# RWKV-7 scan with a gelu MLP on one core: the channels of both halves moved side by side, with one transfer in place of two for three tensors

## The chip, the core and the metric

The kernel runs on one core of a Trainium2 chip. The metric is device microseconds (us) of one execution; lower is better. The page and the views shown come from one profiled execution.

## The reference, cut to what matters

Four sequences (batch B = 4) with eight heads (H = 8) of 40 channels (D = 40) run 768 steps. Each head has a 40 x 40 state, which every step reads, decays and updates; the outputs of the eight heads, 320 numbers for each token, go through an MLP with 2048 hidden units.

```python
for t in range(S):                                   # S = 768
    y[:, :, t] = np.einsum('bhd,bhde->bhe', rt, state)
    Sa = np.einsum('bhde,bhe->bhd', state, at)
    state_decay = state * wt[:, :, None, :] - np.einsum('bhd,bhe->bhde', Sa, bt)
    state = state_decay + np.einsum('bhd,bhe->bhde', vt, kt)
...
x = attn_out.transpose(0, 2, 1, 3).reshape(B * S, H * D)     # 3072 x 320
h = x @ w_in                                                 # 320 x 2048
g = h * (1.0 / (1.0 + np.exp(-1.702 * h)))
return g @ w_out                                             # 2048 x 320
```

## The kernel before

**Units.** Time is cut into 12 chunks of 64 steps, and the batch into two pairs of sequences. A pair in a chunk is a unit; there are 24, i = 0 to 23, with c, p = divmod(i, 2). In a unit the recurrence over 64 steps becomes matrix products: score matrices A, N and RV of 64 x 64 for each head, the inverse of a triangular matrix in five levels (`ps_level`), and products with the state that the unit before left. After the two units of a chunk follows that chunk's MLP: `ps_up`, a gelu on ScalarE (ACT), `ps_down`.

**Halves.** SBUF and PSUM have 128 partitions, and the kernel works on two halves of 64 (`HALF`). The tiles with time on the partitions (`time`, `logw`, `RV`) fill both halves. The tiles with channels on the partitions (`ak`, `b`, `rv`, and the sums `FT`, `GT` of the log decays) use 40 partitions of each half, 0 to 39 and 64 to 103 (`CHANNELS`), one half for the heads with e = 0 and one for those with e = 1. Almost every matmul is a 64 x 64 product that uses one quarter of the array, and `QUARTERS` goes round the four quarters so that four such products run side by side. Everything is fp32, and each product is two records in the trace. All matmuls go through the helper `mm` (L300), so they are told apart by tile: `ps_A`, `ps_N`, `ps_B` and so on.

**Transfers.** All come from the SP queue. For each unit `load` (L495) fetches `ak` (the inputs a and k), `b` and `rv` as two transfers each, of 40 partitions, and `RV` and `time` as one transfer each of 128 partitions; `load_w` (L490) fetches the decays. `part_with` (L967) stores a unit's output `x` to DRAM as two transfers of 40 partitions, and `get_back` (L973) loads it again in the layout of the MLP. `weight` (L429) fetches and converts the weights of the MLP in eight pieces, four transfers each, early in the run.

**Sums of the decays.** For the first four units (`BY_PE = 4`) the sums over time by channel are products on TensorE: `by_channel` (L550) makes 16 products of 64 x 64 with 65 columns (`ps_cumc`). From unit 4 on, VectorE scans make them.

**Products over channels.** `score_A` (L630), `score_N` (L680), the part of `known` (L884) with `zr` and `ak`, and `state_turned` (L857) contract over the 40 partitions of `CHANNELS`.

**Order.** The order of the work is written out by hand: `ORDER` lists all 2700 steps with engine and PSUM bank, and each engine takes its steps in that order. A wait of one step holds back what stands behind it on its engine. In the built program eight semaphores serve the transfers in turn, and the issue of a transfer waits until the one eight places before it has landed; so at most eight are on the way.

Of the kernel before, what the change touches and what calls it, by code (L numbers as in the profile page):

```python
# [107 lines left out]
0s 5s 7s 8s 9s 3a 6s 87p0 88p1 24s 89a1 1s 2s 12s 102a 95d 100p2 90a0 93d 158a 101d2 98p3 96g 10s 94d 17s 97g 16s 99d3 103p1  # L108
4a 11s 132p0 104a1 105d1 142p2 26s 143p3 133a0 106d 130p1 14s 144a3 13s 107p0 15s 18s 151g 108a0 109d0 51s 131a1 110p3 27s
149g 150d 111a3 112d3 159p0 156p1 145a2 161d0 160a0 152g 113p3 345s 92a 162d 25s 153d 114a3 163p2 42s 115d3 34s 19a 274s 264p0  # L110
165d2 265p3 164a2 22d 266a3 166p2 20d 273s 21d 33s 43s 167a2 154p3 168d2 23g 35s 28a 157d1 116p2 155d3 169p1 117a2 118d2 267a0
279d 63s 280g 119p3 277s 171d1 36s 44s 120d3 343s 125d3 278g 124d3 29d 126p2 170a1 123a3 30d 172p1 122a3 127a2 121a 31d 128p2
54s 173a1 287a 288p0 289a0 129d2 32g 174d1 134p3 147s 37a 290d0 175p2 135d3 180a2 146s 178a2 275s 176d2 136p1 179a2 479s 38d
181a2 45s 39d 177a 282g 291d 91s 138a1 182p0 188p3 281d 183a0 186p2 139d 137a1 283p0 187a2 184p1 189a3 40d 276s 292p2 46a
284d0 41g 285p3 185d1 344s 148a 286d3 190p0 293a2 294d2 334p1 335p3 357a 140s 191d0 268g 336a3 315d 192p2 47d 337a1 348d 316p0
194a2 295p3 349d 61s 317a0 195g 60s 347s 358p1 296a3 62s 297d3 360d1 318a0 298p3 271a 361d 319p0 338g 300d3 196s 193a2 320a0
346s 355p2 385d 270s 48d 299a3 362p0 356d2 351g 301p3 363a0 364d0 350g 269s 141s 386p2 197s 302d3 365p0 387a2 352g 359a1 303d3
388a2 323p1 367d0 366a0 321p3 49d 324a1 304p2 322a3 478s 325d1 50g 353p0 309a2 470p3 354d0 209p1 307a2 210p1 310a2 305d2 211p1
308a2 272d 198p0 341a 199p0 72s 212p1 70s 64a 200p0 340s 368p2 52s 342d 339s 69s 201p0 369a2 202p0 370d2 203p0 471a 213p1 65d
214p1 389p2 66d 472a3 483g 204p0 390a2 560s 371p3 67d 306a 53s 215p1 71s 482s 216p1 372a3 217p1 476a 220p2 373d3 68g 218p1  # L120
221p2 477d 219a1 205p0 222p2 206p0 223p2 224p2 207p0 55a 311p3 225p2 79s 312d3 80s 226p2 208a0 58d 313p1 374p3 314d1 227p2 56d
379a3 228p2 229p2 57d 326p0 230a2 59g 393p1 327d0 378a3 391p2 394a1 375d3 231p0 558s 392d2 376a 232p0 233p0 395d1 559s 81s 73a
78s 234p0 480s 381p2 235p0 328p1 481s 382a2 74d 377a3 485d 380a3 236p0 75d 492a 242p2 486d 243p2 82a 76d 484d 77g 383p3 237p0
384d3 244p2 329d1 330d1 488p3 473d 238p0 531d 245p2 487g 246p2 489d3 85d 532p1 239p0 533a1 396p3 331d 332s 474s 475s 534a1
240p0 247p2 397d3 562s 241a0 535p1 83d 490p3 536a1 84d 398p0 572a 491d3 86g 550p1 555s 561s 253p3 399d0 551a 333s 400d0 254p3
401d 402s 554s 255p3 552a1 564d 493p0 705s 556a 567g 570p1 403s 494d0 248p2 563d 566g 249p2 495d0 498d 256p3 571d1 565g 250a2
496a0 251d2 252s 696p1 497g 557d 539p0 537p2 704s 257p3 538a2 540d0 258p3 553d 611d 697a 499d 573p2 784s 700s 259p3 576a2
574d2 710d 260p3 541d0 575d2 404p0 578d 261a3 577g 405p0 579d 698a1 568p2 711g 500p1 406p0 569d2 501a1 407p0 262d3 263s 708s
580p2 702a 502d1 408p0 582d2 409p0 503d 410p0 583d 504a 612p3 411p0 584g 613d3 412p0 614d3 413p0 505p1 709d 414a0 426p3 506d1
427p3 428p3 507d1 429p3 699d 581d2 430p3 615p1 785s 706s 701s 703d 431p3 616a1 585p0 432p3 508d 586a0 433p3 587d0 434p3 509a  # L130
588d 435p3 589d 448p2 436a3 510p1 590p0 511a1 449p2 592d0 591a0 512d1 415p3 513d 416p3 593d 514a 417p3 594g 418p3 515p0 419p3
516a0 517d0 595p1 518d 420p3 596a1 597d1 421p3 598d 422p3 519a 599d 423p3 424p3 520p0 425a3 437p1 521d0 438p1 523d0 522g 439p1
524d0 440p1 525d0 441p1 442p1 526d0 527p3 718p0 929s 528a3 443p1 719d0 787s 444p1 720d0 529p3 445p1 721d0 446p1 530d3 600p0
723d 447a1 542p3 722d 724g 603d0 605a0 619p1 604d0 543d3 450p2 620a1 606d0 544p3 621d1 601d0 602d 617p1 707s 546d3 451p2 618a1
783s 712d 547g 713d 607p0 725p1 608a0 452p2 609p0 453p2 548s 610d0 932s 454p2 727d1 726d1 622p0 728d 545d3 729a 775p1 455p2
623d0 780s 776a 549s 756d 730p3 624p0 456d2 457d2 731d3 458s 459p2 777a1 778g 732d3 786s 788g 781a 779s 626d0 460p2 625d0 627g
733d 795p1 835d 734a 461p2 735p3 791g 462p2 628s 736a3 796d1 737d3 716p0 792g 738d 463p2 782d 739g 1011s 920p1 757p3 925s
464p2 717d0 758a3 629s 759a3 790d 465p2 740p0 789d 466p2 741a0 742d0 921a 797p3 467d2 760p0 1008s 468d2 800a3 923d 652p2 469s
761d0 922a1 653p2 926a 930s 798d3 714p1 799d3 654p2 924s 802d 801g 655p2 934d 803a 656p2 836p0 657p2 715d1 658p2 659p2 837d0
762p3 838d0 927d 660p2 763a3 661p2 764p1 662a2 743d 630p0 744d 928s 631p0 632p0 765d1 804p3 766d1 633p0 805a3 806d3 634p0 807d  # L140
635p0 808a 745p2 636p0 748d2 637p0 749d2 839p1 933g 750d2 638p0 840a1 1009s 751d2 639p0 809p3 746d2 935g 640a0 641p1 810d3
642p1 793p2 747a 811d3 674p0 812d 794d2 813a 752p3 643p1 753a3 814p2 644p1 815a2 816d2 754p3 645p1 755d3 646p1 817d 647p1 818a
767p2 841p3 768d2 648p1 842a3 649p1 819p2 650p1 820a2 821d2 675p0 769p3 822d 651a1 823d 771d3 931s 770d3 772g 824p2 936d 676p0
827a2 828a2 942p1 829a2 677p0 1153s 830a2 937d 945a1 773s 663p3 825d2 664p3 943d1 1156s 826a 665p3 944d1 999p2 947d 946g 666p3
1000a 1004s 980d 940p1 948g 667p3 941d1 668p3 774s 669p3 670p3 831p1 671p3 1001a2 1002d 1003s 832d1 672p3 1005a 1013d 678p0
673a3 1006d 833p2 843p1 679p0 834d2 1007s 844d1 938p2 845d1 680p0 939d2 846p3 681p0 847d3 949p1 1012g 682d0 848p2 950a1 683d0
1014d 684s 685p3 849d2 1015g 1010s 850d2 1021p0 1016g 951d1 686p3 1024a0 1232s 851d 1235s 981p2 687p3 982a2 952d 852s 1022d0
983a2 953g 1144p1 1023d0 688p3 1026d 1145a 1149s 1025d 1027g 984p2 1059d 689p3 1154s 954p0 853s 985a2 1147g 690p3 1158d 1148s
955a0 956d0 986p2 1146a1 957d 1150a 691p3 958d 987a2 1151d 988p0 692p3 989a0 1152s 990d0 959p1 693a3 865p2 960a1 694d3 866p2
961d1 867p2 695s 962d 868p2 963d 1028p0 869p2 1029a0 1030d0 870p2 1031d 1157g 871p2 1159d 1032a 1060p3 872p2 873p2 1061a3  # L150
874p2 1062d3 1033p1 875a2 854p0 1035d1 855p0 1036d 856p0 1037d 1063p3 857p0 1064d3 1034a1 858p0 964p2 859p0 965a2 966d2 1038p1
967d 860p0 1039a1 1040d1 861p0 1041d 1017p3 968a 1042g 862p0 1018d3 863p0 969p2 864a0 876p1 970d2 877p1 972d2 971g 1043p3
973d2 878p1 1044a3 974d2 879p1 975d2 880p1 881p1 1045d3 1019p0 1046d 976p2 1047a 882p1 1020d0 1233s 883p1 977a2 1166p3 884p1
1169a3 1167d3 1377s 978p0 885p1 1168d3 898p2 1171d 1170g 886a1 979d0 887p3 1172a 1048p0 991p1 1051a0 888p3 1052a0 992d1 889p3
1053a0 890p3 1054a0 891p3 1049d0 993p1 1050a 1067p0 994d1 1160g 1155s 892p3 1161d 1068a0 893p3 894p3 1069d0 1380s 895p3 1204d
1065p0 995d1 896p3 996d 1066a0 1231s 1055p1 899p2 897a3 1056d1 997s 1173p0 1223p3 900p2 1174a0 1175d0 1228s 1176d 1224a 1177g
1057p1 901p2 1058d1 1070p0 998s 1164p1 1225a3 1226d 1236g 1227s 1071d0 902p2 1229a 1165d1 1162p3 903p2 1238d 1163d3 904p2
1237d 1178p0 1230d 905p2 1179a0 1180d0 1245p1 906a2 1181d 1072p3 1248a1 1456s 907d2 1182g 1246d1 908s 1247d1 909p0 1250d 1234s
1239g 1073d3 1251a 910p0 1240g 1074d3 1249d 1183p2 1459s 1283d 1368p1 911p0 1184a2 1075d 1373s 912p0 1185d2 1369a 1076s 1186d
1252p3 1187d 913p0 1370a1 1371g 1372s 1382d 1253a3 1188p2 1254d3 1374a 914p0 1255d 1190d2 1256g 1077s 1189a2 1191d 1243p1  # L160
1375d 915p0 1192g 1257p3 916p0 1244d1 1258a3 1259d3 1205p2 917d0 1206a2 1193p1 918d0 1207a2 1089p3 1260d 919s 1196a1 1090p3
# [87 lines left out]
def rwkv7_gelu_quick(ctx: ExitStack, tc: tile.TileContext, time_d, v_d, w_d, wc_d, ak_d, b_d, rv_d, w_in, w_out, out):  # L249
# [12 lines left out]
    WALK = "ebufbub"  # L262
    EARLY = 4
    BY_PE = 4
    PLAIN = 4
    PARTS = 4
    ROUNDS, WINDOW, SHARE = 4, 5000.0, 1.0
    RANKS = [14, 16, 20, 24, 35, 37, 39, 41]
# [97 lines left out]
    for t in logw_t:  # L366
        nc.gpsimd.memset(t[:, DM:], 0.0)
# [770 lines left out]
```

## Time and profile before

| | |
|---|---|
| time, median of 3 runs | 677.02 us (676.87 to 680.05) |
| span of the profiled execution, first to last instruction | 676.5 us |
| PE busy | 648.5 us, 96% of the span |
| PE matmul records | 19488 |
| granted clock of PE, mean | 0.994 |
| DMA | 35313 packets, 69.74 MB |

PE is TensorE's matmuls, PEld its weight loads, DVE VectorE, ACT ScalarE, POOL GpSimd, SP SyncE; SPq is SP's queue of transfer issues. The span was 0.5 us under the median of the runs. "Idle before" is the time for which an engine stood still ahead of an instruction, with what ended it; "issue" there means that the profile shows nothing that was waited for. PEclk is the granted share of TensorE's full clock.

### The profile page before, as it was taken

What the parts mean: (1) busy time and instruction counts of PE and PEld (TensorE: products, weight loads), DVE (VectorE), ACT (ScalarE), POOL (GpSimd) and SP (SyncE); (2) the same over time, 40 slices, a digit from 0 to 9 for tenths busy, and PEclk for the clock granted to TensorE, in tenths of its full rate; (3) what the DMA queues carried; (4) which work ended last, traced back from release to release, by engine and by line L of the source; (5) the groups of instructions that cost most, each with busy time, mean ns of one, the idle gap of its engine ahead of it and who ended that gap; (6) DMA issues with size and microseconds to landing.
All of it is one profiled execution on the core that took longest, in us unless ns stands there. A gap on an engine that the chain in (4) does not pass through costs nothing.

```text
span 676.5 us, 42217 instructions
## 1 busy us (share of the span) xinstructions
PE 648.5 (96%) x19488; PEld 553.4 (82%) x19488; DVE 444.6 (66%) x908; ACT 331.6 (49%) x710; POOL 175.3 (26%) x204
## 2 busy tenths in 40 slices
PE   5768999999999999999999999999999999999997
PEld 5657887987998987788888888798888798798785
DVE  4786787777867667767776587768656766675001
ACT  4676755534564655664545445455454354252110
POOL 6344244224123123123123211322412421300000
PEclk9899999999999999999999999999999999999999
DMA  7983736315314314432404413513412411200200
GB/s 230 300 289 94 232 107 187 103 43 154 108 47 149 93 58 117 121 108 72 118 22 132 141 34 109 156 33 108 140 39 71 122 53 54 61 14 15 61 12 20
DMA packets 35313, 69.74 MB, mean 103 GB/s; under 512 B 5440, under 2 KB 14656, under 8 KB 35136
## 3 DMA queue, kind: packets, MB, share of 16 engines
q1 hardware_dynamic: 35136, 67.03, 32.6%
q8 instruction: 153, 2.51, 1.5%
q14 instruction: 24, 0.20, 0.1%
HBM read 59.15 MB, written 7.86 MB: 99 GB/s over the span
## 4 chain that ended last, share of the span: by engine, by line
PE 93%; DMA 2%; DVE 2%; issue 1%; ACT 1%; DVEq 0%; SPq 0%; ACTq 0%
PE ps_up L300 31%; PE ps_down L300 30%; PE ps_level L300 9%; PE ps_y L300 5%; PE ps_B L300 5%; PE ps_X L300 2%; PE ps_N L300 2%; PE ps_rz L300 2%; PE ps_RV L300 2%; PE ps_A L300 2%; PE ps_zT L300 1%; DMA ak<-in_ak 1%; PE ps_cum L300 1%; PE ps_T L300 1%; DMA b<-in_b 1%
## 5 line engine op out<-in xcount | busy, mean ns | idle before, releaser
L300 PE MATMUL ps_up<-xT_all,w_sb 64*64 64x256 f32 x3840 | 251.0, 377 | 0.8 <-issue 0.4
L300 PE MATMUL ps_down<-w_sb,g 64*64 64x320 f32 x3072 | 237.0, 430 | 0.2 <-ACT zr L877 0.2
L300 PEld LDWEIGHTS ps_up<-xT_all,w_sb 64*64 64x64 f32 x3840 | 170.1, 133 | 15.9 <-issue 1.5
L300 PEld LDWEIGHTS ps_down<-w_sb,g 64*64 64x64 f32 x3072 | 128.0, 133 | 42.8 <-ACT zr L877 0.4
L996 ACT ACTIVATE g<-ps_up 128x1024 f32<-128x1024 f32 x48 | 49.2, 1024 | 45.4 <-PE ps_up L300 45.0
L715 POOL TENSOR_TENSOR EX<-ES,quads 128x512 f32<-128x512 f32 x29 | 38.3, 1322 | 112.7 <-DVE ES L708 74.9
L300 PEld LDWEIGHTS ps_level<-W,EX 64*64 64x64 f32 x2560 | 57.8, 134 | 6.7 <-DVE T L838 0.5
L758 ACT COPY W<-ps_level 128x512 f32<-128x512 f32 (+1 forms) x56 | 29.5, 527 | 67.7 <-PE ps_level L300 65.7
L760 DVE TENSOR_TENSOR E<-two,ps_level 128x256 f32<-128x256 f32 x80 | 33.1, 415 | 34.2 <-ACT W L758 30.1
L300 PE MATMUL ps_level<-W,EX 64*64 64x64 f32 (+1 forms) x2560 | 55.4, 217 | 0.1
L713 ACT ACTIVATE EX<-ES,quads 128x256 f32<-128x256 f32 x80 | 36.3, 501 | 31.0 <-DVE ES L708 30.3
L619 POOL TENSOR_TENSOR ak<-ak,FT 128x512 f32<-128x512 f32 x16 | 20.9, 1305 | 76.6 <-DMA ak<-in_ak 53.4
L708 DVE STREAM_TRANSPOSE ES<-E 128x256 f32<-128x256 f32 x80 | 35.3, 443 | 4.4
L300 PE MATMUL ps_level<-PT,EX 64*64 64x64 f32 (+2 forms) x1280 | 32.8, 235 | 5.1 <-DVE EX L729 3.7
L300 PEld LDWEIGHTS ps_level<-PT,EX 64*64 64x64 f32 x1280 | 30.8, 139 | 8.3 <-DVE EX L729 4.2
L300 PE MATMUL ps_y<-M,bh 64*64 64x104 f32 (+1 forms) x768 | 35.6, 250 | 0.7 <-DVE M L915 0.4
L300 PE MATMUL ps_y<-RV,kh 64*64 64x104 f32 (+1 forms) x768 | 35.6, 251 | 0.0
L899 ACT COPY B<-ps_B 128x416 f32<-128x416 f32 (+1 forms) x34 | 16.6, 492 | 33.4 <-PE ps_B L300 33.2
L300 PEld LDWEIGHTS ps_y<-RV,kh 64*64 64x64 f32 x768 | 28.3, 137 | 2.6 <-DVE M L915 0.5
L689 DVE COPY_PREDICATED PT<-within,ps_N 128x256 f32<-128x256 uint32 x40 | 17.8, 444 | 18.5 <-ACT P L697 13.5
L915 DVE TENSOR_TENSOR M<-ps_X,later 128x832 f32<-128x832 f32 (+1 forms) x24 | 23.8, 993 | 8.3 <-PE ps_X L300 8.1
L300 PE MATMUL ps_B<-RV,A 64*64 64x104 f32 (+1 forms) x768 | 27.9, 252 | 1.1 <-issue 1.1
(131 smaller groups left out, 1088.2 us busy)
## 6 DMA issues: line engine op xcount, KB each, us to landing
ak<-in_ak SPq DMA_DIRECT2D x48, 160.0 KB
rv<-in_rv SPq DMA_DIRECT2D x48, 160.0 KB
time<-in_time SPq DMA_DIRECT2D x24, 320.0 KB
xT_all<-x_dram SPq DMA_DIRECT2D x48, 160.0 KB
wc<-in_wc SPq DMA_DIRECT2D x20, 264.0 KB
logw<-in_w SPq DMA_DIRECT2D x24, 160.0 KB
RV<-in_v SPq DMA_DIRECT2D x24, 160.0 KB
b<-in_b SPq DMA_DIRECT2D x48, 80.0 KB
```

What stands on the lines that cost most here:

```text
L300: nc.tensor.matmul(o, lhsT, rhs, start=start, stop=True, skip_group_check=True)
L619: plan.add(R, {"DVE": 690.0, "POOL": 1270.0, "sbuf": True}, lambda t: of(t.engine).tensor_mul(ahT(), ahT(), FT_of(i)), reads=T("ak", "FT") ...
L689: plan.add(R, dve(256), lambda t, n=n: nc.vector.copy_predicated(tiles_of(at(E0_t, i)), every(within_of(n), [128, 2, 4, 32]), blocks(psum( ...
L708: plan.add(rank, dve(256), lambda t: nc.vector.transpose(ES(n), source(t)), writes=[key("ES", n, 6)], **reads)
L713: nc.scalar.activation(dst[:, :, h], ES(n), ACT.Copy, scale=quads[:, h, :1])
L715: of(t.engine).tensor_mul(dst, ES(n).unsqueeze(2).to_broadcast([128, 8, 2, 32]), quads.unsqueeze(1).to_broadcast([128, 8, 2, 32]))
L758: plan.add(rank, any2(512 - 8 * past), lambda t: copy(t.engine)(tiles_of(W(n + 1))[:, :, :, past:], blocks(psum(t, ""), 64)[:, :, :, past: ...
L760: plan.add(rank, dve(256), lambda t: nc.vector.tensor_sub(tiles_of(E(n + 1)), every(two32, [128, 2, 4, 32]), blocks(psum(t, ""), 64)[:, :, ...
L899: plan.add(R, any2(4 * wide), lambda t: copy(t.engine)(dst(), some(psum(t, "")[:, :, :208])), writes=[("Bv", i)] if x and c > 0 else T("B" ...
L915: plan.add(R + 1, dve(8 * wide), lambda t: nc.vector.tensor_tensor(M_of(i)[:, :, :wide].rearrange("p (j b) n -> p b j n", b=2), some(psum( ...
L996: plan.add(-45, {"ACT": 1030.0, "table": "gelu"}, lambda t: nc.scalar.activation(g_of(c * NQ + q).rearrange("p m r n -> p r m n"), psum(t, ...
```

## The change

The channels of the two halves move next to each other: in `ak`, `b`, the sums of the decays, the state and the output, e = 0 lies on partitions 24 to 63 and e = 1 on 64 to 103 (`MIDDLE`, 80 partitions). The inputs are laid out so on the host. `ak` and `b` are loaded with one transfer of 80 partitions each, and `x` is stored with one. `rv` keeps its place and its two transfers.

Products over channels contract over the whole half of 64 partitions, 24 of which hold zeros in one of the factors. `by_channel` makes 8 products of 64 x 128 in place of 16 of 64 x 64. To have zeros on both sides of the channels, `logw`, `kh`, `bh` and `zT` get gaps of 24 columns, and `kh` and `bh` are written as 4 x 80 columns in place of 8 x 40. The three `logw` buffers become one tile with two fills in place of three.

The order is the same 2700 entries; the text of `ORDER` is only broken into lines at other places. The functions of the MLP were written anew with a switch (`BY_HALF = 0`) that leaves their instructions as they were.

Instruction by instruction, SP issues 342 rows in place of 414 (24 each of `ak`, `b` and `x` go), PE loses 32 products of `ps_cumc` (64 records), POOL one fill, and DVE and ACT keep all theirs. Apart from the waits on transfers no instruction waits for another step than before, but that the first `ps_cumc` product of unit 0, and no longer the sixth, waits for the fill of `logw`.

```diff
+    GAP = 24
+    MIDDLE = slice(GAP, GAP + 2 * D)
...
-    logw_t = several("logw", [128, DM + 24])
-    for t in logw_t:
-        nc.gpsimd.memset(t[:, DM:], 0.0)
+    logw_all = single("logw", [128, plan.slots["logw"] * (GAP + DM) + GAP])
+    by_slot = logw_all[:, :-GAP].rearrange("p (s n) -> p s n", n=GAP + DM)
+    nc.gpsimd.memset(by_slot[:, :, :GAP], 0.0)
+    nc.gpsimd.memset(logw_all[:, -GAP:], 0.0)
...
-    kh_t, bh_t = several("kh", [128, 8, 64]), several("bh", [128, 8, 64])
-    for t in kh_t + bh_t:
-        nc.gpsimd.memset(t[:, :, D:], 0.0)
+    def spaced(name):
+        wide = several(name, [128, 5, 128])
+        for t in wide:
+            nc.gpsimd.memset(t[:, :, :2 * GAP], 0.0)
+        return [t.rearrange("p j n -> p (j n)")[:, GAP:GAP + 512].rearrange("p (j n) -> p j n", n=64) for t in wide]
...
-            rows = [slice(p.start, p.start + D) for p in HALF] if name in ("ak", "b", "rv") else [slice(0, 128)]
+            rows = [MIDDLE] if name in ("ak", "b") else [slice(p.start, p.start + D) for p in HALF] if name == "rv" else [slice(0, 128)]
...
-            for u, f in product(BITS, BITS):
-                for b, e in QUARTERS:
-                    o, h = (2 * u + f) * 65, head(e, f, b, u) * D
-                    mm(ps[HALF[e], b, o:o + 65], logw_t[i % 3][HALF[b], h:h + 64], edges[HALF[b]], o == 0)
+            for u, f, b in product(BITS, BITS, BITS):
+                o, h = (2 * u + f) * 65, head(0, f, b, u) * D
+                mm(ps[:, b, o:o + 65], logw_t[i % 3][HALF[b], h:h + 128], edges[HALF[b]], o == 0)
...
-                    mm(ps[HALF[u], e, o:o + 64], khT()[CHANNELS[e], j], ahT()[CHANNELS[e], j], o == 0)
+                    mm(ps[HALF[u], e, o:o + 64], khT()[HALF[e], j], ahT()[HALF[e], j], o == 0)
...
-                    mm(ps[HALF[b], e, o:o + 64], ahT()[CHANNELS[e], j], b_of(i)[CHANNELS[e], j], o == 0)
+                    mm(ps[HALF[b], e, o:o + 64], ahT()[HALF[e], j], b_of(i)[HALF[e], j], o == 0)
...
-                        mm(ps[CHANNELS[f], e, o:o + D], zr_of(i)[CHANNELS[e], k:k + D], ident[CHANNELS[e], :D], o == 0)
+                        mm(ps[CHANNELS[f], e, o:o + D], zr_of(i)[HALF[e], k:k + D], ident[HALF[e], GAP - GAP * e:GAP - GAP * e + D], o == 0)
...
-                            mm(ps[HALF[b], u, o:o + wide], ahT()[CHANNELS[u], j], both(i)[CHANNELS[u], j, :wide], False)
+                            mm(ps[HALF[b], u, o:o + wide], ahT()[HALF[u], j], both(i)[HALF[u], j, :wide], False)
...
-            for e in BITS:
-                nc.sync.dma_start(rows()[e], x_of()[64 * e:64 * e + D].rearrange("p j b t -> p (j b t)"))
+            nc.sync.dma_start(drams[i].rearrange("(q j) n -> q (j n)", j=4), x_of()[MIDDLE].rearrange("p j b t -> p (j b t)"))
```

More of the change, by code (lines that the diff above doesn't have):

```diff
@@ L112 @@
[L112 to L115, printed above, removed]
@@ L1010, in part @@
                 parts = range(2 * m * DM // PIECE, (2 * (m + 1) * DM - 1) // PIECE + 1)
[L1011 to L1012 removed]
+                plan.add(R + 10 * (p + 1) + m, pe((2, 320)), go, reads=[("gp", (c * NQ + m // 2, p))] + [("weight", NQ + n) for n in parts],
+                         uses=[("g", c * NQ + m // 2)], pair=("down", serial), most=1)
             for m in range(NM):
@@ L1024, in down @@
             plan.add(-100, {"SP": 700.0}, store, reads=[("ob", serial), ("out", serial)], size=128 * DM * 4)
-        for q in range(NQ):
+        for q, ps in product(range(NQ), groups):
             for m in BITS:
                 for k in range(NK):
-                    up(q, m, k)
-            gelu(q)
+                    up(q, m, k, ps)
+            gelu(q, ps)
         for p in BITS:
@@ L1077, in time_tile, with channel_tile @@
         return t.reshape(len(units), 128, H * D)
-    def channel_tile(x, half, order):
+    def channel_tile(x, half, order, middle=True):
         x = np.asarray(x, np.float32).reshape(B, H, NC, C, D)
@@ L1087, in channel_tile @@
                 h = at["e"] + 2 * at["f"] + 4 * (at["b"] ^ at["u"])
-                t[n, at[half], :D, slot] = x[2 * p + at["b"], h, c].T
+                lead = 24 * (middle and not at[half])
+                t[n, at[half], lead:lead + D, slot] = x[2 * p + at["b"], h, c].T
         return t.reshape(len(units), 128, 8, C)
```

328 lines of the change are left out of this document (173 added, 155 removed).

## The prediction

> **What bounds the kernel now.** I read the page from the top, then busy time by stretch, then the first 70 us as a timeline.
>
> ```profile
> PE 648.5 (96%) x19488; PEld 553.4 (82%) x19488; DVE 444.6 (66%) x908; ACT 331.6 (49%) x710; POOL 175.3 (26%) x204
> PE   5768999999999999999999999999999999999997
> DMA  7983736315314314432404413513412411200200
> PE 93%; DMA 2%; DVE 2%; issue 1%; ACT 1%; DVEq 0%; SPq 0%; ACTq 0%
> ```
>
> PE is the chain that ended last, for 93% of the span. It has gaps only in the first four of the 40 slices (17 us each), where DMA is at 7 to 9 tenths. Busy time by stretch (PE, PEld, DVE, ACT, POOL, then granted clock, DMA share, GB/s) says it more finely:
>
> ```profile
> 5.00:10.00 5.00, 2.81 (x79) 2.24 (x72) 2.02 (x3) 2.38 (x11) 4.30 (x19) 1.00 0.95 273
> 35.00:40.00 5.00, 2.94 (x128) 2.60 (x128) 4.93 (x7) 4.14 (x11) 2.64 (x2) 1.00 0.96 296
> 45.00:50.00 5.00, 2.89 (x126) 2.61 (x127) 3.66 (x7) 2.85 (x5) 3.15 (x2) 1.00 0.91 300
> 50.00:55.00 5.00, 4.79 (x162) 4.76 (x165) 2.31 (x4) 2.49 (x11) 0.02 (x1) 0.66 0.08 30
> 120.00:300.00 180.00, 179.71 (x5622) 154.22 (x5618) 129.31 (x272) 100.14 (x209) 47.63 (x51) 1.00 0.33 98
> 300.00:500.00 200.00, 200.00 (x6145) 169.72 (x6141) 142.33 (x302) 97.86 (x200) 50.13 (x54) 1.00 0.32 96
> ```
>
> From 120 to 500 us PE is idle for 0.29 of 380 us. There an earlier transfer, a shorter SP queue or a lighter POOL is worth nothing; only the pace of the matmuls counts. All that the 72 removed transfers can bring lies before about 70 us: in the stretches shown PE works under 3 of 5 us there, and the DMA share is above 0.9.
>
> **Transfers.** The list of issues by tile has 14 groups with 412 issues:
>
> ```profile
> DMA packets 35313, 69.74 MB, mean 103 GB/s; under 512 B 5440, under 2 KB 14656, under 8 KB 35136
> ...
> ak<-in_ak SPq DMA_DIRECT2D x48, 160.0 KB
> rv<-in_rv SPq DMA_DIRECT2D x48, 160.0 KB
> ...
> b<-in_b SPq DMA_DIRECT2D x48, 80.0 KB
> ...
> x_dram<-x SPq DMA_DIRECT2D x48, 80.0 KB
> ...
> xT_all<-in_w_out SPq DMA_DIRECT2D x4, 320.0 KB
> ```
>
> The smallest data row is 1280 bytes, so the 5440 packets under 512 B are marks of completion, one for each DMA engine that took part. The four groups shown with x48 (192 issues) have 40 rows, the other 220 have 64 or 128. 220 x 16 is 3520, and the remaining 1920 are 10 for each of the 192. So a transfer of 40 rows uses ten engines, four rows on each, and six get nothing. The Trainium skill ("DMA: Bandwidth & Descriptors", section on why a DMA increments its semaphore by 16) states the rule: the largest count up to 16 that divides the rows. By it 80 rows use all sixteen; no row of this trace shows 80.
>
> What this costs is read from SP's issues, since an issue waits for the landing of the transfer eight before it. The order is `logw`, two `ak`, two `rv`, `RV`, `time`, two `b`, then:
>
> ```profile
> 5.17 0.35 SPq L469 DMA_DIRECT2D w_sb<-in_w_in  x1
> 6.02 1.29 SPq L492 DMA_DIRECT2D logw<-in_w  x2
> 7.98 0.68 SPq L503 DMA_DIRECT2D rv<-in_rv  x2
> 9.23 0.76 SPq L503 DMA_DIRECT2D ak<-in_ak  x2
> 10.24 1.24 SPq L469 DMA_DIRECT2D extra<-in_w_in  x2
> ```
>
> So the first half of `ak` has landed at 5.17, the second at 6.02, the second of `rv` at 7.98, `time` at 9.23, the second of `b` at 10.24. A half of `ak` (160 KB, 40 rows) takes 0.85 us; `RV` and `time` (480 KB, 128 rows) take 1.25, which is 0.42 for 160 KB; the two of `b` (160 KB together) take 1.01. As one transfer on sixteen engines `ak` would take 0.83 in place of 1.70 (gain 0.87) and `b` 0.42 in place of 1.01 (gain 0.59). If 80 rows stay on ten engines, both gains are nil. I take the sixteen, since the transfers with 64 rows and those with 128, on either side of 80, use sixteen. The same page's rules say of two transfers to disjoint halves that they serialize because both go to all sixteen engines; here they share ten, so merging brings more than that rule allows.
>
> **The first unit.** Who waits:
>
> ```profile
> 8.01 1.02 PE L300 MATMUL ps_RV<-rv 40*64 40x64 f32 x27 [0.53 <-DMA rv<-in_rv]
> 9.27 0.69 DVE L650 TENSOR_TENSOR RV<-ps_RV,upper 128x512 f32<-128x512 f32 x1 [1.25 <-PE ps_RV L300]
> 10.25 0.78 DVE L621 SCALAR_TENSOR_TENSOR b<-b,GT 128x512 f32<-128x512 f32 x1 [0.29 <-DMA b<-in_b]
> 11.29 0.49 PE L300 MATMUL ps_N<-b,ak 40*64 40x64 f32 x8 [1.30 <-DVE b L621]
> 11.42 0.47 ACT L526 ACTIVATE logw<-logw 128x320 f32<-128x320 f32 x1 [3.60 <-DMA logw<-in_w]
> 16.03 1.26 POOL L624 TENSOR_TENSOR ak<-ak,GT 128x512 f32<-128x512 f32 x1 [4.28 <-DMA ak<-in_ak]
> 18.48 0.69 DVE L621 SCALAR_TENSOR_TENSOR b<-b,GT 128x512 f32<-128x512 f32 x1 [0.22 <-DMA b<-in_b]
> ```
>
> `rv` keeps its form but lands 0.87 earlier behind `ak`; so the product L650 runs from 8.40 to 9.09. `b` lands 0.87 + 0.59 earlier, at 8.8. Now L650, ahead of it on DVE, is late: L621 starts at 9.1 instead of 10.25, and `ps_N` of unit 0 moves by 1.15 us (bounds 0 and 1.46). What comes next also waits for transfers, and they move by at least that: `logw` of unit 1 by 1.46, its `ak` by 2.33 (another 0.87), its `b` by 2.92. From there to 44 us the pace is a relay of PE, ACT and DVE (DVE 4.93 of 5 us between 35 and 40), so the 1.15 us is carried on and does not grow, though transfers run further ahead.
>
> **The sums by channel.** Four units, 16 products to 8:
>
> ```profile
> L300 PE MATMUL ps_cumc<-edges,logw 64*64 64x65 f32 x128 | 4.5, 291 | 0.6 <-DVE EX L729 0.6
> L300 PEld LDWEIGHTS ps_cumc<-edges,logw 64*64 64x64 f32 x128 | 4.3, 200 | 0.9 <-DVE EX L729 0.9
> ```
>
> Two products run side by side in place of four, so the columns streamed one after another are as many as before; only the issue of 16 records in each unit goes. At 4.5 us of busy time for 128 records, half of it is 2.2 us for the four units, and the work of units 0 and 2 lies before waits for `b` and for DVE's transposes: at most 1.1 us gained. Against it: the Trainium skill ("TensorEngine Tiling (Array Packing)", Key Properties) says that a change of tiling mode drains TensorE, and a 64 x 128 product amid 64 x 64 ones is two such changes for each unit. By that rule, at one record and one weight load for a change, the sum would lose about 2.0 us in units 1 and 3. From the rows: a change cannot cost less than nothing nor more than a record and its load, 0.49 us, and two units have four of them, 2.0 us. I take 0.3 us gained, near the end that the count of records gives, since the array is half empty here anyway. Bounds: 1.1 gained, 2.0 lost.
>
> **What costs nothing, and its cover.** Contraction over 64 rows:
>
> ```profile
> L300 PE MATMUL ps_A<-ak 40*64 40x64 f32 x768 | 17.7, 222 | 1.6 <-ACT QT L824 0.8 <-issue 0.5 <-ACT wch L569 0.3
> L300 PE MATMUL ps_Q<-ES,P 64*64 64x64 f32 x384 | 11.0, 218 | 0.6 <-DVE ES L708 0.6
> L300 PE MATMUL ps_B<-zr,ak 40*64 40x104 f32 x640 | 23.0, 249 | 0.0
> L300 PE MATMUL ps_B<-RV,A 64*64 64x104 f32 x704 | 26.2, 256 | 1.1 <-issue 1.1
> L393 POOL MEMSET kh<- 128x192 f32 x2 | 0.5, 258 | 0.0
> ```
>
> With 64 columns 40 rows take 222 ns and 64 rows 218, with 104 columns 249 and 256: the columns set it, so nothing (bounds 4 ns less and 7 ns more for a record). The four fills of `kh` and `bh` grow from 192 to 240 columns, by 0.26 us on POOL, in front of the first `kh`; POOL then idles 4.28 us ahead of L624, which covers it. The products for `kh` and `bh` keep their 320 elements. The 24 stores of `x` shorten an already hidden way.
>
> **The sum.** 1.15 + 0.3 is 1.45 us off a span of 676.5, so 675.05; the median of the runs was 0.5 above that span, so 675.5 us, with 674.0 to 677.0 as this case's own range. A measurement of this kernel tells about 0.5%, 3.4 us, from no change; that is below 673.6 or above 680.4. The forecast is a small gain inside it.
>
> **Rivals.** Two turn on one place:
>
> ```profile
> 50.21 0.51 PE L300 MATMUL ps_cum<-logw,edges 64*64 64x160 f32 x3 [2.13 <-issue]
> ```
>
> PE stands still for 2.13 us with nothing shown that it waits for, and goes on just as the burst of transfers ends (DMA share 0.91 before 50 us, 0.08 after). Then the granted clock is 0.66 for 5 us, a loss of 1.7. Together 3.8 us.
>
> Faster: the stall and the slow clock go, 675.5 - 3.8 = 671.7. If the queue stayed full throughout, four `ak` (0.87) and five `b` (0.59) would end the burst 6.4 us sooner; PE, 1.5 us earlier itself, finds it over if 3.6 of these come true. Against: SP also waits for computing steps, which move by 1.5 only. Chance 0.32.
>
> Slower: such a stall comes once more. The profile ties it to no step, and with other transfers and 64 records fewer it falls elsewhere; between 50 and 70 us PE is dense enough to pay for it. Each costs 3.8: with one more 679.3, with two 683.1; slower by over 0.5% from the second on. Against: fewer transfers compete. Chance 0.13, of which 0.08 for two.
>
> No gain: 80 rows are no faster, or the relay of the engines hides it: 677.0, or up to 679 with the drains. Chance 0.10.
>
> Contraction over 64 rows is slower after all. `ps_A` and `ps_N` have 16 products in each of 24 units, `ps_B` (with `zr`) and `ps_zT` in 22, at two records each: 2944 records, so 2.9 us for each ns; from 1.7 ns on slower by over 0.5%. At the 7 ns above it would be 695, but the stretches without idle time would have to lengthen. Chance 0.05.
>
> **How the numbers follow.** The forecast has 0.40. Faster by over 0.5%: the first rival and 0.02 of the forecast's tail, 0.34. Slower: 0.08 + 0.05 = 0.13. The rest is 0.53. The range from 671.2 to 680.0 takes in the forecast, the first rival, no gain and one more stall; outside are two stalls, the slower contraction and about 0.05 below.
>
> **What would show it.** Right: completion marks near 5440 - 192 x 10 + 48 x 10 + 72 x 16 = 5152, L621 of unit 0 at about 9.1 and `ps_N` at 10.1, PE idle before 70 us less by 1 to 2 us, busy time from 120 to 500 us as before. Wrong: 4720 marks (80 rows on ten engines), L621 still at 10.2, a mean over 222 ns for `ps_A`, or a stall on "issue" that has gone or doubled.

## The result and the profile after

The changed kernel took 685.45 us (median of 4 runs, 683.87 to 687.18) where the kernel before took 677.70 beside it: a ratio of 1.0101, 95% interval 1.0070 to 1.0132. On a second chip the ratio was 1.0078 (1.0054 to 1.0103). So it is slower by 5 to 8 us; the forecast was 675.5 with a range up to 680.0, and "slower by over 0.5%" had a chance of 0.13.

The lines of the page after that answer to those shown of before (the row that begins with "q8" is that of a DMA queue: packets, MB, share of the engines):

```profile
PE 655.5 (96%) x19424; PEld 581.8 (85%) x19424; DVE 443.2 (65%) x908; ACT 331.8 (48%) x710; POOL 173.8 (25%) x203
PE   6677999999999999999999999999999999999997
DMA  8974746315314414431404513513412412101100
DMA packets 35022, 69.71 MB, mean 102 GB/s; under 512 B 5152, under 2 KB 14368, under 8 KB 34848
q8 instruction: 153, 2.51, 1.5%
PE 93%; issue 2%; ACT 2%; DVE 2%; DMA 0%; DVEq 0%; ACTq 0%
```

PE is busy 7 us longer with 64 records fewer. The marks of completion are 5152, as predicted for 80 rows on sixteen engines. "issue" in the chain went from 1 to 2%. Busy time by stretch (PE, PEld, DVE, ACT, POOL, granted clock, DMA share, GB/s):

```profile
5.00:10.00 5.00, 3.89 (x78) 3.40 (x76) 2.28 (x4) 2.39 (x11) 4.30 (x19) 1.00 1.02 305
35.00:40.00 5.00, 4.19 (x107) 3.38 (x111) 3.83 (x9) 2.45 (x10) 0.19 (x1) 0.50 1.05 304
45.00:50.00 5.00, 2.80 (x128) 2.40 (x126) 4.58 (x11) 4.43 (x11) 1.57 (x2) 1.00 0.34 102
50.00:55.00 5.00, 4.13 (x127) 3.48 (x127) 4.00 (x7) 3.51 (x13) 2.42 (x2) 1.00 0.79 266
120.00:300.00 180.00, 179.56 (x5539) 160.29 (x5533) 129.90 (x273) 96.86 (x205) 47.33 (x50) 1.00 0.33 95
300.00:500.00 200.00, 199.44 (x6092) 176.53 (x6088) 140.13 (x299) 98.73 (x203) 49.73 (x55) 1.00 0.34 99
```

The burst of transfers does not end sooner (share 0.79 between 50 and 55 us). In the last two rows PE is idle for 1.00 of 380 us, against 0.29 before: by this view next to nothing is lost there.

The records of a tile come in the same order in both kernels, so the n-th record of before can be set against the n-th of after. In the two profiled executions the first `ps_A` is 0.35 us late, the 33rd `ps_N` (unit 1) 0.8, the 385th `ps_up` (at 124.6 us before) 3.8, and the last record 8.0. Half is lost in the first 125 us, half after, where the view of the stretches shows no room for it. The first half does not begin at the start: the records that the kernel before starts at 31 us come 0.4 us early in the changed kernel, those that it starts at 34 us come 3.6 us late. A second execution of the changed kernel (in the second set below), set against the kernel before with 64 rows on the same chip, shows the same: 1.3 us early, then 1.0 us late.

**What stands behind "issue".** On PE after (start, duration, engine, line, operation, then the idle time before it):

```profile
34.89 0.33 PE L310 MATMUL ps_level<-PT,EX 64*64 64x32 f32 x4 [2.58 <-issue]
41.55 0.77 PE L310 MATMUL ps_X<-B,T 64*64 64x104 f32 x24 [0.49 <-issue]
46.47 0.25 PE L310 MATMUL ps_y<-M,bh 64*64 64x104 f32 x1 [1.47 <-issue]
55.46 0.31 PE L310 MATMUL ps_y<-M,bh 64*64 64x104 f32 x2 [1.23 <-issue]
59.22 0.46 PE L310 MATMUL ps_N<-b,ak 64*64 64x64 f32 x14 [1.16 <-issue]
```

All five stand in the middle of a step, between two products of the same tile, where there is no data to wait for. The packets of queue q8 explain them. There are 153, of 2.51 MB, so 16.4 KB each; PE's 38848 records and loads divided by 153 are 254, or 127 matmul records for a packet; the 284 semaphore and drain instructions between them bring it to 255.8. The Trainium skill ("Trainium Architecture — The Big Picture", The software stack) gives an instruction 64 bytes: 256 in 16 KB, and the trace agrees; that they are put into the engine when the program is loaded, the trace does not bear out, since the packets run all through the execution. From the records of the trace:

```
number of the record    601    728    855    981   1108   1234   1362   1490   1616   1870
PE starts it at       34.89  41.55  46.47  50.10  55.46  59.22  62.70  66.97  70.75  80.29
q8 packet starts      32.45  38.75  44.22  47.71  52.92  56.86  60.37  64.38  68.17  78.00
q8 packet has landed  33.56  40.06  45.16  48.65  53.84  57.87  61.30  65.53  69.33  78.97
```

The stalls lie 127 records apart (one end, near record 1743, passes without), at the ends of the blocks of instructions, and PE goes on 1.3 to 1.6 us after a packet has landed, 2.3 to 2.8 us after it started. The 2.13 us stall of before, which the prediction could tie to no step, is record 1107: packet from 47.94 to 48.90, PE goes on at 50.21. So PE is refilled in blocks of 127 records, and stands where it reaches the end of a block sooner than about 2.3 us after the next refill has started. After 100 us the longest such pauses are 0.3 to 0.7 us; most of that is covered by the four products still under way, so it hardly shows as idle time.

That much of the later loss stands at these ends can be read record against record. After 125 us the changed kernel falls back by another 4.2 us. Cut each block into eighths of 16 records: 3.5 of the 4.2 us arise in the first eighth of its own blocks, and in the first eighth of the blocks of the kernel before it catches up by 1.0. In the second execution the same reckoning gives only 0.7 of 2.1 us.

### The profile page after: what moved, and what is told of

Its sections match the earlier page's. It is cut to its first block, busy times and chain, and to the rows that moved or that the text cites. A ratio compares the mean times of both kernels' runs of the same rounds, so it can differ in the third digit from the quotient of the medians.

```text
span 684.5 us, 41937 instructions
## 1 busy us (share of the span) xinstructions
PE 655.5 (96%) x19424; PEld 581.8 (85%) x19424; DVE 443.2 (65%) x908; ACT 331.8 (48%) x710; POOL 173.8 (25%) x203
## 2 busy tenths in 40 slices
DMA packets 35022, 69.71 MB, mean 102 GB/s; under 512 B 5152, under 2 KB 14368, under 8 KB 34848
## 3 DMA queue, kind: packets, MB, share of 16 engines
q8 instruction: 153, 2.51, 1.5%
## 4 chain that ended last, share of the span: by engine, by line
PE 93%; issue 2%; ACT 2%; DVE 2%; DMA 0%; DVEq 0%; ACTq 0%
PE ps_up L310 31%; PE ps_down L310 30%; PE ps_level L310 9%; PE ps_y L310 5%; PE ps_B L310 5%; PE ps_X L310 3%; PE ps_N L310 2%; PE ps_A L310 2%; PE ps_rz L310 2%; PE ps_RV L310 1%; PE ps_zT L310 1%; PE ps_cum L310 1%; PE ps_T L310 1%; PE ps_Q L310 1%; ACT PT L809 1%
## 5 line engine op out<-in xcount | busy, mean ns | idle before, releaser
L310 PE MATMUL ps_up<-xT_all,w_sb 64*64 64x256 f32 x3840 | 257.1, 378 | 1.2 <-issue 0.7
L310 PE MATMUL ps_down<-w_sb,g 64*64 64x320 f32 x3072 | 244.3, 430 | 0.2 <-ACT zr L894 0.2
L310 PEld LDWEIGHTS ps_up<-xT_all,w_sb 64*64 64x64 f32 x3840 | 172.6, 133 | 19.6 <-issue 3.8
L310 PEld LDWEIGHTS ps_down<-w_sb,g 64*64 64x64 f32 x3072 | 153.3, 133 | 23.6 <-issue 0.4
L310 PEld LDWEIGHTS ps_level<-W,EX 64*64 64x64 f32 x2560 | 61.4, 134 | 4.7 <-DVE T L855 0.5
L310 PE MATMUL ps_level<-W,EX 64*64 64x64 f32 (+1 forms) x2560 | 58.2, 217 | 0.1
L310 PEld LDWEIGHTS ps_y<-RV,kh 64*64 64x64 f32 x768 | 30.8, 133 | 2.3 <-issue 0.6
L310 PEld LDWEIGHTS ps_y<-M,bh 64*64 64x64 f32 x768 | 29.3, 133 | 2.1 <-issue 1.4
```

The lines of the kernel that those rows point to most:

```text
L310: nc.tensor.matmul(o, lhsT, rhs, start=start, stop=True, skip_group_check=True)
```

## The experiments

The changes were undone and made one by one, and spare products were used to move the ends of the blocks. Times are set against the kernel before on the same chip; the chips differ by nearly as much as the change (the kernel before: 676.7 to 681.4 us). In the forecasts R is the theory of the block ends, T that of the transfers on all sixteen DMA engines, C that of the products over 64 rows and the spaced tiles.

**First set.** The kernel before took 681.3 us on this chip, 3.6 us more than on the first, for which the forecasts in us were made. The sums undone:

```diff
-            for u, f, b in product(BITS, BITS, BITS):
-                o, h = (2 * u + f) * 65, head(0, f, b, u) * D
-                mm(ps[:, b, o:o + 65], logw_t[i % 3][HALF[b], h:h + 128], edges[HALF[b]], o == 0)
+            for u, f in product(BITS, BITS):
+                for b, e in QUARTERS:
+                    o, h = (2 * u + f) * 65, head(0, f, b, u) * D + 64 * e
+                    mm(ps[HALF[e], b, o:o + 65], logw_t[i % 3][HALF[b], h:h + 64], edges[HALF[b]], o == 0)
```

> The changed kernel, with the sums by channel as 16 products of 64x64 for each unit again (so PE has its 19488 records back); all the rest as changed. Three theories for the 8 us. Block ends (R): PE gets its own instructions in 16 KB blocks, one for about 127 matmul records; it stands still where it reaches the end of a block less than about 2.3 us after the transfer of the next has started, and the 64 records fewer have moved the ends of the blocks by half a block to worse places; besides, the 64x128 products cost about 1 us for each of the first units. R expects 676 to 679 us, and stalls inside of steps after 100 us as rare as in the kernel before. Transfers (T): the 80-row transfers use all 16 DMA engines, so the blocks of instructions start late; T expects about 683 to 684, since only the cost of the products goes. Contraction and strides (C): the products over 64 rows and the spaced kh, bh and zT are slower; C expects about 683 to 684.

Measured: 1.0072 (1.0037 to 1.0106), 684.84 us. A part comes back at best; R was wrong here.

Spare products, in the changed kernel and in the kernel before, n = 32:

```diff
+    spare = banks.tile([128, 2, 512], FP32, tag="pair3", name="ps_spare")
+    for n in range(32):
+        r, h = QUARTERS[n % 4]
+        mm(spare[HALF[h], r, :8], ident[HALF[r]], ident[HALF[r], :8], True)
     for t in tasks:
         t.fn(t)
```

> The changed kernel with 32 spare products (64 records, 8 columns each, into PSUM columns that are overwritten) at the very start, where PE has nothing to do until 3.7 us. They do nothing but move all later records back by half a block of instructions. R expects that the loss after 100 us (4.6 us) goes and the cost of the sums stays: 679 to 682. T and C expect 685 to 686.5, the changed kernel's time and up to 1 us for the spare products.

Measured: 1.0051 (1.0029 to 1.0073). Work was added, and it was if anything faster than the changed kernel elsewhere (1.0101 and 1.0078).

> The kernel before with the same 32 spare products (64 records) at the very start; nothing else differs. Half a block more moves the ends of the blocks to the same places of the program as half a block less. R expects 681 to 685, with stalls inside of steps after 100 us as in the changed kernel. T and C expect 677 to 678.5.

Measured: 1.0128 (1.0099 to 1.0158), 8 to 9 us, somewhat more than R had. Thirty-two products that compute nothing, at a time when PE has nothing to do, cost the kernel before as much as the whole change. T and C cannot give that. Against the profile of the kernel before, the execution profiled here falls back by 8.0 us after 125 us, 5.4 of them in the first eighth of its blocks.

The transfers undone:

```diff
-            rows = [MIDDLE] if name in ("ak", "b") else ...
+            rows = [slice(24, 64), slice(64, 104)] if name in ("ak", "b") else ...
...
-            nc.sync.dma_start(drams[i]..., x_of()[MIDDLE]...)
+            for e in BITS:
+                nc.sync.dma_start(drams[i]...[e], x_of()[GAP + D * e:GAP + D * (e + 1)]...)
```

> The changed kernel with ak, b and x moved as two transfers of 40 rows each again (rows 24 to 63 and 64 to 103), everything else as changed. T expects 678 to 680: the refills of PE's instructions find engines free again. R and C expect 684 to 686.5; R adds that the stalls stay at the same record numbers.

Measured: 1.0149 (1.0109 to 1.0188), 691.64 us. Not faster; T as the single cause falls. It is above R's forecast too: with the wide products kept, two transfers are if anything slower than one (the changed kernel has 1.0101 and 1.0078 on other chips, and only the second interval is clear of this one).

**Second set, another chip.** In the kernel before, `CHANNELS` becomes `HALF` in the operands of `score_A`, `score_N`, `known` and `state_turned`:

```diff
-                    mm(..., khT()[CHANNELS[e], j], ahT()[CHANNELS[e], j], o == 0)
+                    mm(..., khT()[HALF[e], j], ahT()[HALF[e], j], o == 0)
```

> The kernel before, with the four products over channels contracting over the whole 64 partitions of each half (the 24 above the channels hold zeros), as the changed kernel does; layout, transfers, sums and the number of records stay. C (the products over 64 rows are slower) expects 2.9 us for each ns, so 680 to 690 if C is to carry a good part of the 8 us, that is 0.4 to 1.9% above the kernel before. R (ends of the blocks of instructions) and T expect no difference, under 0.25%.

Measured: 0.9996 (0.9979 to 1.0012). C falls. The changed kernel's groups say the same:

```profile
L310 PE MATMUL ps_B<-zr,ak 64*64 64x104 f32 x640 | 24.1, 250 | 0.2 <-issue 0.2
L310 PE MATMUL ps_A<-ak 64*64 64x64 f32 x768 | 17.9, 223 | 2.2 <-issue 0.9 <-DVE ak L636 0.8 <-ACT wch L586 0.3
```

A record takes 250 ns and 223 where with 40 rows it took 249 and 222.

The spare products of the kernel before in other numbers (n = 64 and n = 16), and the changed kernel beside them:

> The kernel before with 64 spare products (128 records, 8 columns each) at the very start: a whole block of instructions, so the block ends come to within one record of where they were in the program. R expects what the kernel before takes and up to 2 us for the spare products themselves, 0 to 0.3% above, well below the kernel with 64 spare records (1.3% above). If the spare records do harm by themselves (a cold start, a later first product), it is slower than with 64: 1.3 to 2.5% above.

> The kernel before with 16 spare products (32 records): a quarter of a block. R expects a place of its own between the kernel before and the one with 64 spare records, 0.2 to 1.5% above. If only the number of spare records counts, half of 1.3%: 0.6 to 0.7%.

> The changed kernel, unaltered, beside the others on one chip: 1.0% above the kernel before (0.7 to 1.3%), by every theory.

Measured: with 128 spare records 1.0040 (1.0021 to 1.0059), with 32 records 1.0052 (1.0031 to 1.0074), the changed kernel 1.0078 (1.0054 to 1.0103). Over 0, 32, 64 and 128 records the time goes 1, 1.005, 1.013 (this one on the chip of the first set), 1.004: it rises to half a block and falls again towards a whole one, though not quite to nothing as R had it. The number of spare products alone cannot give that; the place of the block ends can.

**Third set.** Both undone (the layout alone is left), beside the sums undone alone:

> The changed kernel with the sums as 64x64 products and with ak, b and x as two transfers of 40 rows each: of the change only the layout is left (places of the channels, gaps in logw, kh, bh and zT, 64 rows). The block ends are those of the kernel before. If the merged transfers are what is still slow with the sums undone, this is the kernel before again, -0.2 to 0.25%. If the layout is (L: spaced weights and state read at other places), it stays 0.5 to 0.9% above.

> The changed kernel with the sums as 64x64 products, as once before, beside the kernel of the layout alone on one chip; the only difference between the two is the merging of the transfers. R and what it gains in the first unit expect -0.1 to 0.3% against the kernel before; what was measured on another chip was 0.7% (0.4 to 1.1).

Measured: 1.0019 (0.9993 to 1.0045) for the layout alone, 1.0049 (1.0023 to 1.0074) with the merged transfers. The means of the 12 runs each are 2.1 us apart, with 1.4 us of uncertainty: beside sums of 64x64 merging costs, where the forecast had it gain 1.15.

Then the wait of the refills themselves:

```diff
-            plan.add(rank, {"SP": 350.0}, lambda t, some=some: nc.sync.dma_start(raw()[:, some], src[:, some]),
-                     reads=before, ...)
+            def fetch(t, some=some):
+                for n in range(2):
+                    part = slice(some.start + n * PIECE // PARTS // 2, some.start + (n + 1) * PIECE // PARTS // 2)
+                    nc.sync.dma_start(raw()[:, part], src[:, part])
+            plan.add(rank, {"SP": 350.0}, fetch, reads=before, ...)
```

> The kernel before with each of the 32 transfers of weights cut into two of half the columns (160 KB), so fewer bytes are on the way at a time while SP waits for the eighth last. If the refills of PE's instructions wait behind data that is already on the way (Q), they start earlier in the first 75 us (2.0 us after PE has entered a block in the kernel before; 1.2 to 1.6 expected), and the time falls by 0.2 to 0.7%. If their late start has another cause, the lateness stays and the time moves by less than 0.2%, or rises for the 32 more issues.

> The changed kernel with the weights' transfers cut in two in the same way. Q expects 2.3 us of lateness to fall to 1.4 to 1.8 and 0.2 to 0.8% less time than the changed kernel, 0.1 to 0.8% above the kernel before. Otherwise it stays 0.8 to 1.0% above.

Measured: 1.0012 (0.9990 to 1.0035) and 1.0117 (1.0073 to 1.0162). The mechanism of Q holds and its gain does not. In the kernel before the mean lateness of the refills in the first 75 us fell from 1.9 to 1.2 us, and the stalls on them (pauses of over 0.26 us at a block end that end 1.2 to 1.7 us after a landing, 12 to 100 us) from 8.0 us in eight places to 2.1 in three. But the 385th `ps_up` came only 0.35 us sooner than in the profile of the kernel before. In the changed kernel the lateness fell from 2.3 to 1.5 us, and it was no faster. The waits of PE between 28 and 100 us (us in total, times, longest), first before, then with the transfers cut:

```profile
PE ps_cum L300 <- issue: 2.1, 1, 2.1
PE ps_level L300 <- DVE EX L729: 2.0, 2, 1.2
PE ps_X L300 <- DVE T L838: 1.2, 1, 1.2
PE ps_B L300 <- issue: 1.1, 1, 1.1
PE ps_T L300 <- ACT QT L824: 0.9, 1, 0.9
PE ps_A L300 <- ACT QT L824: 0.8, 1, 0.8
PE ps_rz L300 <- issue: 0.8, 1, 0.8
```

```profile
PE ps_level L300 <- DVE EX L732: 2.4, 3, 1.3
PE ps_cum L300 <- ACT logw L529: 1.8, 1, 1.8
PE ps_A L300 <- ACT QT L827: 1.5, 1, 1.5
PE ps_X L300 <- DVE T L841: 1.4, 2, 1.1
PE ps_T L300 <- ACT QT L827: 0.9, 1, 0.9
PE ps_Q L300 <- DVE ES L711: 0.8, 1, 0.8
PE ps_B L300 <- issue: 0.7, 1, 0.7
```

The `ps_cum` whose fourth record stood 2.1 us on "issue" now stands 1.8 us on ACT's `logw` ahead of its first record. In the start-up a stall that goes is largely replaced by waits that were hidden under it.

**Fourth set.** The 64x128 products kept, and 16 spare records behind them in each of the four units:

```diff
                 mm(ps[:, b, o:o + 65], logw_t[i % 3][HALF[b], h:h + 128], edges[HALF[b]], o == 0)
+            for n in range(8):
+                r, h = QUARTERS[n % 4]
+                mm(ps[HALF[h], r, 272:280], ident[HALF[r]], ident[HALF[r], :8], True)
```

> The changed kernel with 16 spare records (8 columns each) behind the 64x128 products of each of the first four units, so that every later record has the number that it has in the kernel before, from the first unit on. Against the changed kernel only the block ends move; against the kernel with 64x64 sums (0.5 and 0.7% above the kernel before) only the price of the 64x128 products is left. R expects 0.3 to 0.8% above the kernel before, with most of the changed kernel's 3 us at 125 us of the run gone. If the 64x128 products are the cause in the first 100 us (S), it stays as the changed kernel: 0.8 to 1.1% above, and 3 us late at 125 us.

Measured: 1.0091 (1.0057 to 1.0124). The record numbers of before alone do not bring the time back, as S has it. But the spare records are not free here: a unit's products for the sums now take 2.51 us cold, for 1.97 in the changed kernel and 1.12 in the kernel before. With the spare records at the start it was 1.0051; the two intervals meet, and what is left to the block ends and what to the 64x128 products cannot be told from these.

Transfers of 32 and 48 rows in place of 40 and 40, beside the layout alone:

```diff
-slice(24, 64), slice(64, 104)
+slice(24, 56), slice(56, 104)
```

> The kernel of the layout alone, with ak, b and x cut into transfers of 32 and 48 rows in place of 40 and 40: the same number of transfers and bytes, but each on 16 DMA engines in place of ten. If it is the engines that the merged transfers add which make the refills of PE late (E), the refills after 100 us start 0.1 to 0.2 us later than in the layout alone and it is 0.2 to 0.5% slower than that. If merging costs for another reason, or nothing, both are equal within 0.2%.

> The kernel of the layout alone again, beside the one above on the same chip: -0.1 to 0.3% against the kernel before by every theory.

Measured: 1.0030 (1.0011 to 1.0050) and 1.0011 (0.9987 to 1.0035). The difference has the sign of E but is within the uncertainty, and in the two profiled executions the refills after 100 us were later in the second (0.79 and 0.88 us), against E. Not decided.

> The kernel before with 64 spare records at the start, on another chip (1.3% above on the first). R expects 0.6 to 1.4% above, more than with 32 (0.5%) and with 128 (0.4%). If the first chip was the cause, it comes to 0.2 to 0.5%, between those two.

Measured: 1.0102 (1.0077 to 1.0128). Half a block costs 1% on this chip too. Against the profile of the kernel before, 4.1 of the 5.2 us lost after 125 us arise in the first eighth of a block.

**Fifth set.** With the sums undone, the merged transfers in the first four units only, and in the others only:

```diff
-            rows = [MIDDLE] if name in ("ak", "b") else ...
+            rows = ([MIDDLE] if i < 4 else [slice(24, 64), slice(64, 104)]) if name in ("ak", "b") else ...
```

and the same for `x`; for the second kernel `i >= 4`.

> The kernel with 64x64 sums, ak, b and x merged for the first four units alone and as two transfers of 40 rows from unit 4 on. Merged everywhere it was 0.5 and 0.7% above the kernel before, merged nowhere 0.1 and 0.2%. If merging costs where PE has no idle time (D), this keeps the gain of the first unit and loses the rest: -0.1 to 0.2%, and it is the best of all. If it costs in the start-up (U), this is as the kernel merged everywhere: 0.4 to 0.7%.

> The other half: ak, b and x merged from unit 4 on, as two transfers of 40 rows for the first four units. D expects 0.4 to 0.7% above the kernel before, U 0.0 to 0.25%.

Measured: 1.0010 (0.9987 to 1.0033) and 1.0038 (1.0018 to 1.0058). This fits D: merging neither gains nor costs where it was to bring a gain, and from unit 4 on, where it was to bring nothing, the kernel is 0.4% (2.6 us) above the kernel before, of which the layout may have 0.1 to 0.2%. The two kernels' means are 1.6 us apart, with 1.5 us of uncertainty, so the difference between them is barely clear. No version beats the kernel before: the layout alone, 64 rows alone, the halved transfers and the merging in the first four units have 1 inside their intervals.

## Why the prediction was wrong, point by point

**What bounds the kernel.** That PE is the bound was right. The step that failed is the next: from 0.29 us of idle time in 380 it concluded that after 120 us only the pace of the matmuls counts, so transfers could neither gain nor lose there. Of the 8 us 4.2 were lost after 125 us, 3.5 of these just behind the block ends, and 64 spare records at the start cost the kernel before 1.0 and 1.3% with the work after them unchanged. PE's own instructions come through the DMA engines as well, and a refill that is late lets PE run dry for some tenths of a microsecond, under products that are drawn as busy. The prediction's sum has no term for this: the 64 records that go were counted only as work saved. Between 300 and 500 us after, PE is idle for 0.56 us; but from the 1025th `ps_down` record (298.4 us before) to the 2049th (497.5) the changed kernel took 200.4 us for 199.1. One execution is little for that: the layout alone, on other chips, took 201.8 and 202.8.

**Transfers.** The rule was right: 5152 marks. The landings, read from the issues that wait for them, are right in part: `rv` 7.13 for 7.98 (0.85 earlier, 0.87 predicted), the issue behind `b` 9.17 for 10.24 (1.07, 1.46 predicted). Two cautions. The 5.17 from which the prediction reckons 0.85 us for half of `ak` is no landing: that issue follows the one before it (4.79, 0.33 us long) at SP's own pace, so the half had landed by then, and what it took cannot be read. And executions differ: with the layout alone, on one chip with the sums undone, the two landings are 7.46 and 9.59 for 7.30 and 9.38, so there merging brought 0.2 us.

**The first unit.**

```profile
9.53 1.06 DVE L638 SCALAR_TENSOR_TENSOR b<-b,GT 128x512 f32<-128x512 f32 x1
10.84 1.13 PE L310 MATMUL ps_N<-b,ak 64*64 64x64 f32 x32 [0.64 <-DVE b L638]
```

L638 (L621 before) starts at 9.53, not 9.1, and `ps_N` is 0.45 us earlier, not 1.15. With the sums undone it is nearly what was predicted:

```profile
9.39 0.69 DVE L639 SCALAR_TENSOR_TENSOR b<-b,GT 128x512 f32<-128x512 f32 x1
10.33 1.14 PE L310 MATMUL ps_N<-b,ak 64*64 64x64 f32 x32 [1.03 <-DVE b L639]
```

0.96 us. Over the executions profiled `ps_N` starts at 10.31 to 10.46 with merged transfers and 64x64 sums (three) and at 10.55 to 11.48 with two transfers and no spare records (six), so the size was near, with some luck in the pair; on one chip it is 10.33 for 10.55. What failed is "carried on to 44 us". At the 385th `ps_up` the three with an earlier first unit (sums undone, twice; merged in the first four units) stand 0.7, 7.3 and 1.3 us behind the kernel before, the first of them 0.2 us behind the layout alone on its own chip, and merging there is worth nothing (1.0010). The start-up waits on other things by then.

**The sums by channel.** The products take longer, where the forecast had 0.3 us gained. The products of units 0, 1 and 2 (start, duration), before and after:

```profile
4.24 1.12 PE L300 MATMUL ps_cumc<-edges,logw 64*64 64x65 f32 x32
13.39 1.12 PE L300 MATMUL ps_cumc<-edges,logw 64*64 64x65 f32 x32
24.93 0.69 PE L300 MATMUL ps_cumc<-edges,logw 64*64 64x65 f32 x32 [0.57 <-DVE EX L729]
```

```profile
4.46 1.97 PE L310 MATMUL ps_cumc<-edges,logw 64*128 64x65 f32 x16
13.13 1.97 PE L310 MATMUL ps_cumc<-edges,logw 64*128 64x65 f32 x16
25.11 1.11 PE L310 MATMUL ps_cumc<-edges,logw 64*128 64x65 f32 x16 [0.24 <-DVE EX L746]
```

Half the records take 0.85, 0.85 and 0.42 us longer (unit 3 cannot be compared, since the kernel before runs it at the half clock). The reason given was that two side by side stream as many columns as four did; left out was the weight load. In unit 0 a pair of loads starts at 4.62, its products at 4.73, the next loads at 4.83: load and product take turns, 213 ns for two records, where before four records took 107 with the loads of one quarter under the products of the others. By the Trainium skill's rule ("TensorEngine Tiling (Array Packing)", Key Properties), weighed in the prediction, it is the changes of mode that drain; here the first pair takes 57 ns more than the others, and all the rest of the loss lies within the mode. The exponential of `FT` starts at 6.47 for 5.44: the cover named for unit 0 (waits for `b`) does not hold 1 us. What this comes to at the end is not shown: as said above, the changed kernel is level or ahead at 31 us, behind three of the four units, and falls back at the stall that follows; the kernel with spare records among these products stands 2.0 us behind the layout alone on its chip at 30 us.

**What costs nothing.** Right: 64 rows, the fills, the spaced `kh`, `bh` and `zT`. The layout alone is 1.0019 and 1.0011, both with 1 inside the interval.

**The rivals.** "Slower: such a stall comes once more" named the right place and half of the reason ("with 64 records fewer it falls elsewhere"), but gave it 0.13 and took the place to be open. It is bound to record numbers: any change in the count of records in front of a dense stretch moves all block ends behind it, and this one moved them by half a block. "Faster: the stall and the slow clock go" was wrong in kind: with 6 us of stalls taken away nothing was gained.

**What the 8 us are.** Against the kernel before, the layout is 0.1 to 0.2% (none is possible), and the layout with merged transfers 0.5 to 0.7%. The whole change is 0.8 to 1.0%; so with merged transfers the 64x128 products, and the block ends that they move, add up to 0.5%. But the parts do not simply add. Without merged transfers the same products bring it from 0.1 to 0.2% to 1.5%, on different chips, so merging seems to cost beside 64x64 sums and to gain beside 64x128 ones. A price found by undoing one part holds only with the others as they are. Shown are the size of the layout, the longer products, that half a block costs 1% by itself in the kernel before, and that in the first comparison most of the loss after 125 us stands at block ends. Two things stay open: how the rest divides, and why merging costs beside 64x64 sums. Later refills would fit, but the two kernels that should have shown it did not differ enough.

## What to carry to other kernels

Where PE runs without idle time, look at the count of instructions and at the queue that carries them: a step that adds or removes records moves every later end of a block, and its price is then that of the new places, whatever the step was for. Before a term is forecast at "nothing", try on the chip what spare instructions in the same number do: here they moved the time by 1%, and a change worth less than that cannot be judged by its time alone. Undo the parts of a change in more than one order, since here they did not add. A wider product is not cheaper by its columns when its weight load was hidden before and is not any more.

## What the runs showed of the hardware that was not expected

- PE's instructions arrive during the run in packets of 16.4 KB, one for 127 matmul records; PE starts the first record of a block at the earliest 2.2 to 2.3 us after its packet has started. If the semaphore instructions are counted too, the ends lie 256 instructions apart, and at the same counts in all twenty executions profiled. After 100 us a refill starts 0.5 to 0.9 us after PE has entered a block (means of the executions); in the first 75 us, where the DMA share is above 0.9 in several of the stretches of 5 us, up to 6.5 us after.
- The chips differ in it: on that of the second set a refill took 1.02 to 1.03 us in the mean and the kernel before 676.7 us; on that of the first comparison 1.05 to 1.07 and 677.7; in the other sets 1.11 to 1.15 and 680.2 to 681.4.
- One program on one chip spreads by 1% over its runs (the kernel before 677.0 to 684.6 in the first set), so the profile of one execution tells mechanisms, and only many runs tell a half per cent.
- Leaving out the last 5 us of the run, the half clock is recorded in stretches of 3.41 us or multiples of it and not at the same places: 3.4 us in all in the second execution of the changed kernel, 6.8 in the first, 20.5 in that of the kernel before with 64 rows, which was none the slower. The Trainium skill ("TensorE: Matmul & The Clock Gate", What's actually happening) has a free-running window of that length; the trace agrees with the length.
